# A fused attention and MLP kernel: the opening's three stages written as one list of steps, with some loads on another queue

## The chip, the cores and the metric

The kernel runs on one core of one Trainium2 chip. The metric is the device time of one execution in microseconds. Each time here is that of a whole run, or comes from the trace of one profiled execution, whose times count from the span's start.

## The reference

For 8 batches, 12 heads, 448 tokens and head size 64, cosine attention is followed by a two-layer MLP over the 3584 x 768 result:

```python
q_n = q / (np.linalg.norm(q, axis=-1, keepdims=True) + 1e-06)
k_n = k / (np.linalg.norm(k, axis=-1, keepdims=True) + 1e-06)
attn = softmax(np.matmul(q_n, k_n.transpose(0, 1, 3, 2)) / tau)
x = np.matmul(attn, v)        # heads side by side: 3584 x 768
h = x @ w_in                  # 768 x 2048
g = 0.5 * h * (1.0 + erf(h * inv_sqrt2))
return g @ w_out              # 2048 x 768
```

Inputs and output are float32; the matmuls take bf16 operands.

## The kernel before

**Work and tiles.** Four heads of a batch make a group: 3 groups a batch, 24 in all. Group 0 is split in two, so there are 25 *units*: units 0 and 1 are the halves of group 0, unit u is group u - 1 from there. A group's tokens lie as 7 chunks of 64 tokens, its heads as two pairs.

For each unit, q and k are loaded (`load_qk`, L126), squared (`square`, L151), summed over the head size on VectorE (`reduce`, L162), turned into inverse norms by a logarithm, an exponential and a reciprocal (`logs` L172, `roots` L177, `inverses` L182), multiplied by them on GpSimd into a bf16 tile (`scale`, L196), and turned round (`transposes`, L210): for the first five units on TensorE, with a copy from PSUM by VectorE (`copies`, L223), for all others by a DMA transpose on SyncE's queue. Q and K name the halves. A unit's scale can't start before its norms are there; `groups` (L117) says which units' norms are worked out together: units 5 and 6 (groups 4 and 5) share one logarithm and root.

Then come scores (`scores`, L232) into a pair of PSUM banks, exponentials on ScalarE (`exps`, L246; a visit is scores and exponential of one chunk for both head pairs, `visit`, L654), column sums by a matmul with ones (`sums`, L298), the matmul with v (`values`, L324), and the normalising into x (`turned` L341, `inverted` L346, `spread` L362, `normalise` L367).

A batch's x, 768 x 448, goes through the first layer as 16 tiles of 6 matmuls each (`w_in`, L467; tiles "hp", contraction steps kd 0 to 5, two for each group), then GELU on ScalarE into g. The second layer (`second_pieces`, L397) is a list of pieces of one matmul each (384 columns; 16 to a tile), which is used as filling between the score visits of the next batch; VectorE copies the finished tile and SyncE stores it.

**Order.** `manual_schedule` (L69) takes the program's order as each engine's order, so each engine and each queue works strictly down its own list, and waits for data and buffers only. A DMA is issued by the engine whose queue it is on: SP loads q and k and stores the output; GpSimd's queue loads v, w_in and w_out, converting to bf16 (`load_v` L141, `load_wi` L436, `load_wo` L445). `upto(f, n)` (L454) calls f for all units below n that it has not yet been called for.

The first batch has an order written out by hand, `attention_first` (L472). The first layer of each batch is `first(b)` (L863), which also holds next units' preparation; the attention of batches 1 and up is `attention(b, fill)` (L702), with a branch of its own for batch 1 (L740) and for batch 2 (L770). The counts in `parts` say how many second-layer pieces stand between visits. ScalarE needs other tables for GELU than for exponentials, so a table load stands at each change (`preload_act_table_set`).

**PSUM.** Eight banks: two single ones by turns (`mm_tile`, L102, shared by transposes, projections, pieces and fillers), two pairs for scores, and two for sums and values of the first batch, which become a third pair behind it (L961 to 963). A tile in a bank that is still being read makes TensorE wait. `qkp` has 4 buffers, so group 4's load takes group 0's.

**Fillers.** `spin(n)` (L460) is n matmuls on blank data. Before the first transposes there are 20 of them (L952) and 2 more (L495); seven others stand among the transposes, scores and the start of the first layer.

**The opening's loads.** All loads of groups 0 to 3 are issued on SP at the start, but for one on ScalarE's queue. `late` (L954) is a small copy on GpSimd that waits for group 0's last load, and so holds back GpSimd's queue. Groups 4 and 5 are loaded by SP at L507 and L535. In `attention_first` one first-layer tile, hp 4, gets its first two matmuls early (L632).

Of the kernel before, what the change touches and what calls it, by code (L numbers as in the profile page):

```python
# [16 lines left out]
def kernel(  # L17
# [17 lines left out]
    nc = tc.nc  # L35
# [90 lines left out]
    def load_qk(g):  # L126
# [137 lines left out]

    def gathered(g, p):
# [58 lines left out]
    def values(g, chunks=range(C), p=None):  # L324
        for c in chunks:
            if c == 0 and g < NQ:
# [70 lines left out]
    def second_pieces(sb, t, ni):  # L397
        state = {}

        def mm(kf):  # L400
# [8 lines left out]
            if kf == KF - 1:  # L409
                nc.vector.tensor_copy(ot[:, ni * NH:(ni + 1) * NH], ps[:, :NH])  # L410
# [7 lines left out]
        return [lambda kf=kf: mm(kf) for kf in range(KF)]  # L418
# [46 lines left out]
    early = {}  # L465

# [5 lines left out]
    def attention_first():  # L472
        x_t[0] = xp.tile([128, KD, S], BF16, tag="x", name="x0")
        DV, AC, GP = nc.vector, nc.scalar, nc.gpsimd
        Q, K = 0, 1
        square(0, ((AC, Q),))
        square(0, ((AC, K),))
        reduce(0, Q)
        reduce(0, K)
        square(1, ((AC, Q),))  # L480
        upto(load_v, 1)
        logs(0)
        reduce(1, Q)
        roots(0)
        upto(load_wi, 1)
        square(1, ((AC, K),))
        inverses(0)
        square(2, ((AC, Q),))
        reduce(1, K)
        scale(0, ((GP, 1),))  # L490
        logs(1)
        reduce(2, Q)
        roots(1)
        scale(0, ((GP, 0),))
        spin(2)  # L495
        transposes(0, 1)
        square(2, ((AC, K),))
        inverses(1)
        spin(1)
        transposes(0, 0)  # L500
        square(3, ((AC, Q),))
        copies(0, 1)
        scale(1, ((GP, 0),))
        copies(0, 0)
        square(3, ((AC, K),))
        scale(1, ((GP, 1),))
        upto(load_qk, 5)  # L507
        spin(1)
        transposes(1, 0)
        reduce(2, K)  # L510
        scores(0, ((0, 0), (0, 1)))
        upto(load_v, 2)
        transposes(1, 1)
        copies(1, 0)
        logs(2)
        scores(0, ((0, 2), (0, 3)))
        roots(2)
        upto(load_wi, 2)
        exps(0, ((0, 0), (0, 1)))
        inverses(2)  # L520
        copies(1, 1)
        exps(0, ((0, 2), (0, 3)))
        spin(2)
        scores(0, ((0, 4), (0, 5)))
        scale(2, ((GP, 0),))
        reduce(3, Q)
        exps(0, ((0, 4), (0, 5)))
        spin(1)
# [482 lines left out]
```

## Time and profile before

| what | us |
|---|---|
| median of 3 runs | 400.88 |
| the runs | 400.53, 400.88, 407.3 |
| span of the profiled execution | 398.6 |
| the median above that span | 2.28 |
| TensorE busy | 392.0 |
| ScalarE busy | 267.8 |
| VectorE busy | 264.0 |
| GpSimd busy | 250.6 |

No separate time is recorded for the profiled execution beside its span, so the 2.28 us stand for what lies around the span.

TensorE's matmuls overlap, so a busy TensorE is not always at its best; the pitch from one matmul to the next says more. In the chain that ended last each line gives the start, the length and the work. In the timeline each line gives the start, the length, the engine (PE matmul, PEld weight load, DVE VectorE, ACT ScalarE, POOL GpSimd, SPq the DMA issues of SyncE), the source line, the operation with its tiles and count, and in brackets the idle time ahead of it with what ended it. A row of DMA issues gives the size and the time from issue to landing.

### The profile page before, as it was taken

Reading aid. Unit: us, or ns where it says so; the run is one execution under the profiler, and the core shown is the slowest. Engines: PE = TensorE matmul, PEld = TensorE weight load, DVE = VectorE, ACT = ScalarE, POOL = GpSimd, SP = SyncE. Lnnn points to the kernel's source line nnn. Section 1 sums busy time; section 2 is a strip of 40 time slices with the busy share of each in tenths; the row PEclk is TensorE's granted clock in tenths of the full one; section 3 lists DMA queues with packets and bytes.
Section 4 is the critical chain, followed back from the end, with each engine's and each line's share of the span. In section 5 each row is a group of like instructions: output and inputs, shape, how many; then the busy total and the mean of one; then the engine's idle time right before and its main releaser. Section 6 shows DMA issues by size and latency. Waiting matters only on the chain.

```text
span 398.6 us, 8027 instructions
## 1 busy us (share of the span) xinstructions
PE 392.0 (98%) x3245; PEld 207.8 (52%) x3245; DVE 264.0 (66%) x530; ACT 267.8 (67%) x399; POOL 250.6 (63%) x162
## 2 busy tenths in 40 slices
PE   7999999999999999999999999999999999999996
PEld 3444555555545555555555555555555555555564
DVE  5787214955487999589963999769973797461021
ACT  6995787557988877888665977889656756504300
POOL 5898814269699694959587394969768391920000
PEclk9999999999999999999999999999999999999999
DMA  8999999747296890678145591566024720130033
GB/s 290 261 258 217 205 233 308 154 106 226 50 254 234 158 230 2 178 150 207 70 105 138 126 240 38 162 113 147 2 27 101 148 46 2 41 77 3 1 80 80
DMA packets 66485, 54.52 MB, mean 137 GB/s; under 512 B 38672, under 2 KB 62352, under 8 KB 66448
## 3 DMA queue, kind: packets, MB, share of 16 engines
q1 hardware_dynamic: 54464, 41.79, 39.0%
q0 software_dynamic: 11600, 11.80, 18.8%
q8 instruction: 25, 0.41, 0.4%
q10 hardware_dynamic: 384, 0.43, 0.3%
q14 instruction: 12, 0.10, 0.1%
HBM read 45.61 MB, written 11.01 MB: 142 GB/s over the span
## 4 chain that ended last, share of the span: by engine, by line
PE 95%; issue 1%; DVE 1%; POOL 1%; ACT 0%; POOLq 0%
PE hp L469 37%; PE op L406 36%; PE st L242 9%; PE o L320 4%; PE o L335 4%; PE op L425 1%; PE sm L305 1%; PE sh L667 1%; PE tp L221 1%; PE sm L314 1%; PE spin L463 0%; POOL wi L441 0%; DVE nq L168 0%; POOL qkb L204 0%; POOL v L145 0%
## 5 line engine op out<-in xcount | busy, mean ns | idle before, releaser
L252 ACT ACTIVATE pt<-st 128x896 bf16<-128x896 f32 x155 | 132.5, 916 | 29.0 <-PE st L242 28.4
L406 PE MATMUL op<-wo,g 128*128 128x384 bf16 x864 | 148.1, 326 | 0.0
L469 PE MATMUL hp<-x,wi 128*128 128x448 bf16 x768 | 147.0, 353 | 0.1
L204 POOL TENSOR_TENSOR qkb<-qk,rn 128x896 bf16<-128x896 f32 (+1 forms) x50 | 80.2, 1628 | 66.3 <-DVE rn L188 64.9
L406 PEld LDWEIGHTS <-g 128*128 128x128 bf16 x864 | 81.4, 98 | 62.6 <-issue 11.2
L469 PEld LDWEIGHTS <-wi 128*128 128x128 bf16 x768 | 74.4, 98 | 71.1 <-issue 2.8
L263 POOL TENSOR_TENSOR acc<-acc,pt 128x896 f32<-128x896 f32 x55 | 103.8, 1887 | 4.3
L929 ACT ACTIVATE g<-hp 128x448 bf16<-128x448 f32 x128 | 63.6, 552 | 63.6 <-PE hp L469 63.5
L410 DVE COPY ot<-op 128x384 f32<-128x384 f32 x54 | 29.9, 555 | 83.1 <-PE op L406 80.8
L168 DVE TENSOR_REDUCE nq<-sq 128x14 f32<-128x896 f32 (+1 forms) x50 | 50.6, 1038 | 10.2 <-POOL sq L160 6.7
L242 PE MATMUL st<-qkT 64*64 64x448 bf16 x620 | 46.0, 356 | 0.2 <-ACT pt L252 0.2
L160 POOL TENSOR_TENSOR sq<-qk 128x896 f32<-128x896 f32 x18 | 29.9, 1683 | 16.3 <-DMA qk<-in_q_dram 10.9
L369 DVE TENSOR_TENSOR x<-o,rs 128x448 bf16<-128x448 f32 x48 | 28.0, 609 | 9.9 <-PE sh L667 6.4
L270 DVE TENSOR_TENSOR acc<-acc,pt 128x896 f32<-128x896 f32 x30 | 33.0, 1099 | 1.0
L158 ACT ACTIVATE sq<-qk 128x896 f32<-128x896 f32 (+1 forms) x32 | 27.8, 902 | 2.2 <-DMA qk<-in_q_dram 1.8
L364 DVE STREAM_TRANSPOSE rs<-rc 128x448 f32<-128x448 f32 x48 | 28.7, 626 | 0.6
L242 PEld LDWEIGHTS <-qkT 64*64 64x64 bf16 x620 | 17.9, 105 | 20.5 <-issue 12.7
L263 POOL TENSOR_TENSOR acc<-pt 128x896 f32<-128x896 bf16 x11 | 20.7, 1879 | 8.9 <-DVE x L369 8.9
L320 PE MATMUL o<-pt,v 64*64 64x448 bf16 x364 | 24.2, 351 | 0.0
L673 ACT ACTIVATE pt<-sh 128x448 bf16<-128x448 f32 x26 | 14.1, 544 | 9.2 <-PE sh L667 8.5
L276 DVE STREAM_TRANSPOSE ta<-acc 128x448 f32<-128x448 f32 x32 | 18.5, 617 | 0.2
L335 PE MATMUL o<-pt,v 64*64 64x448 bf16 x308 | 17.5, 351 | 0.5 <-DVE x L369 0.5
(54 smaller groups left out, 212.4 us busy)
## 6 DMA issues: line engine op xcount, KB each, us to landing
qk<-in_q_dram SPq DMA_DIRECT2D x23, 448.0 KB, 4.6
qk<-in_k_dram SPq DMA_DIRECT2D x23, 448.0 KB, 5.4
out_dram<-ot SPq DMA_DIRECT2D x48, 192.0 KB, 3.2
v<-in_v_dram POOLq DMA_DIRECT2D x7, 672.0 KB, 7.7
wo<-in_moe_w_out_dram POOLq DMA_DIRECT2D x4, 768.0 KB, 11.6
wi<-in_moe_w_in_dram POOLq DMA_DIRECT2D x4, 512.0 KB, 14.4
out_dram<-ot SPq DMA_DIRECT2D x12, 96.0 KB, 2.1
wi<-in_moe_w_in_dram POOLq DMA_DIRECT2D x4, 256.0 KB, 14.6
```

The lines of the kernel that those rows point to most:

```text
L160: eng.tensor_tensor(sq, t, t, ALU.mult)
L168: nc.vector.tensor_reduce(nq_t[n][:, j, i], sq_t[g, i][:, s0:s1], mybir.AxisListType.X, ALU.add)
L204: eng.tensor_tensor(qkb[:, i, :, s0:s1].rearrange("p c s d -> p s c d"), t[:, i, s0:s1], rn[:, i].to_broadcast([128, s1 - s0, C, D]), ALU. ...
L242: nc.tensor.matmul(st[cols, n, :S], lhsT=qkT[rows, 1, c, cols], rhs=qkT[rows, 0, :, cols], start=True, stop=True, tile_position=(64 * s, 6 ...
L252: nc.scalar.activation(pt, st[:, :, :S], AF.Exp, scale=inv_tau)
L263: nc.gpsimd.tensor_tensor(acc_t[g], all_t[g][:, 0] if c == 1 else acc_t[g], all_t[g][:, c], ALU.add)
L270: nc.vector.tensor_tensor(acc_t[g], acc_t[g], all_t[g][:, c], ALU.add)
L320: nc.tensor.matmul(bank_t[g, h][64 * s:64 * (s + 1), :S], lhsT=v_t[g][rows, s, c, :], rhs=pt_t[g, s, c][rows], start=(c == 0), stop=(c == ...
L335: nc.tensor.matmul(bank_t[g, h][cols, :S], lhsT=v_t[g][rows, s, c, :], rhs=pt_t[g, s, c][rows], start=(c == 0), stop=(c == C - 1), tile_po ...
L406: nc.tensor.matmul(ps[:, :NH], lhsT=g_t[sb][:, kf, t * 128:(t + 1) * 128], rhs=wo[:, kf, ni * NH:(ni + 1) * NH], start=(kf == 0), stop=(kf ...
L469: nc.tensor.matmul(t, lhsT=wi[:, kd, m * 128:(m + 1) * 128], rhs=x_t[b][:, kd, :], start=(kd == 0), stop=(kd == KD - 1))
L929: nc.scalar.activation(g_t[sb][:, m, hf * S:(hf + 1) * S], hps.pop(m), AF.Gelu)
```

## The change

`attention_first`, the branches of `attention` for batches 1 and 2, and what `first` did for batches 0 and 1, are replaced by one function `opening()` of 594 steps, which calls the same helpers one at a time. The work is the same; what differs is the order in which each engine meets it. `first` and `attention` serve the later batches as before.

What moves, so far as the prediction speaks of it: 28 fillers (29 before), all ahead of the first transposes. The q half of unit 1 is squared on GpSimd instead of ScalarE. v is loaded behind the first part of w_in; w_in's parts come in the order 0, 2, 1, 3. `late_copy` stands behind the squares of unit 4. Groups 5 and 4 are loaded through ScalarE's queue, behind the batch's last exponential. Unit 5 (group 4) is squared on ScalarE, ahead of the first GELU, unit 6 on GpSimd. w_out's four loads are spread out. First-layer tiles 1, 0 and 2 get their banks ahead of the last sums of group 2, tile 0 in the bank that held a value tile; tile 1 also gets two matmuls there. In batch 0's first layer the GELUs come in another order than the tiles. Later, group 6's load, its square and unit 6's scale follow each other as shown.

```diff
-    def load_qk(g):
+    def load_qk(g, queue=None):
...
-                eng = nc.scalar if g == 0 and s0 == 0 and i == 1 else nc.sync
+                eng = queue or (nc.scalar if g == 0 and s0 == 0 and i == 1 else nc.sync)
...
+    def opening():
+        load_qk(0)
+        x_t[0] = xp.tile([128, KD, S], BF16, tag="x", name="x0")
+        square(1, ((GP, Q),))
+        spin(2)
+        spin(20)
+        spin(2)
+        table(EXP_SET)
+        square(0, ((AC, Q),))
+        reduce(0, Q)
+        square(0, ((AC, K),))
+        reduce(0, K)
+        square(1, ((AC, K),))
+        logs(0)
+        roots(0)
+        spin(1)
+        spin(1)
+        spin(1)
+        spin(1)
+        reduce(1, Q)
+        load_wi(0)
...
+        inverses(1)
+        scale(0, ((GP, 0),))
+        transposes(0, 0)
+        copies(0, 0)
+        load_qk(2)
+        scale(0, ((GP, 1),))
...
+        transposes(0, 1)
+        copies(0, 1)
...
+        reduce(2, K)
+        logs(2)
+        roots(2)
+        copies(1, 1)
+        load_v(0)
+        exps(0, ((0, 0), (0, 1)))
+        load_v(1)
...
+        values(1, (6,))
+        scores(2, ((0, 4), (1, 4)))
...
+        mm(0, 1, 0, 2)
...
+        logs(4)
+        roots(4)
+        exps(2, ((0, 6), (1, 6)))
...
+        values(2, (6,))
+        inverted(1)
+        load_qk(5, AC)
+        spread(1, 0)
+        banks(0, 3, 0)
+        table(GELU_SET)
+        load_qk(4, AC)
...
+        sums(2, (5,))
+        sums(2, (6,))
+        mm(0, 0, 0, 2)
...
+        square(5, ((AC, Q),))
+        square(6, ((GP, Q),))
...
+        gelu(0, 1)
+        gelu(0, 2)
+        mm(0, 5, 2, 4)
+        load_wo(1)
+        mm(0, 5, 4, 6)
+        square(5, ((AC, K),))
...
+        mm(0, 9, 2, 4)
+        transposes(4, 0)
...
+        gelu(0, 6)
...
+        table(EXP_SET)
+        logs(5)
+        roots(5)
...
+        table(GELU_SET)
...
+        inverses(5)
+        scale(5, ((GP, K),))
...
+        table(EXP_SET)
+        visit(0)
+        visit(1)
+        scale(5, ((GP, Q),))
+        visit(2)
+        run(1)
+        load_wo(2)
...
+        transposes(5)
...
+        load_qk(6)
...
+        square(7, ((AC, Q),))
...
+        load_wo(3)
+        visit(1)
+        square(7, ((GP, K),))
+        run(17)
+        scale(6, ((GP, Q),))
...
+        scale(6, ((GP, K),))
...
+        transposes(6)
+        run(3)
+        visit(1)
```

In this list `mm(b, m, k0, k1)` are the matmuls of tile m with contraction steps k0 to k1, `bank` and `banks` give tiles their PSUM banks, `run(n)` takes n second-layer pieces, `table` loads a ScalarE table, and `normalise`, `reduce` and the rest are the helpers named above.

More of the change, by code (lines that the diff above doesn't have):

```diff
@@ new lines, in attention @@
+        upto(scale, u + 5)
+        upto(transposes, u + 5)
+        upto(load_qk, g0 + 9)
+        mixed(g0, 0, (1,), (2, 1))
+        squared(u + 6, 0)
+        folded(g0 + 2, range(3))
+        run()
+        for h in range(2):
+            spread(g0 + 1, h)
+        if b + 1 < B:
+            visit(2, 0, 1)
+        else:
+            visit(2, 0)
+            weighted(g0 + 1, 1)
+            visit(2)
+        folded(g0 + 2, range(3, 6))
+        run()
+        for i in range(2):
+            reduced(u + 5, i)
@@ L884, in first @@
             bank(m)
[L885 to L898 removed]
+            mm(m, range(KD - 2))
+        if b + 1 < B:
             for n in range(3, 5):
```

939 lines of the change are left out of this document (577 added, 362 removed).

## The prediction

> **What bounds the kernel now.** I read the totals first, then the chain that ended last in order of time, then the opening instruction by instruction, then the DMA rows. The totals:
> ```profile
> span 398.6 us, 8027 instructions
> PE 392.0 (98%) x3245; PEld 207.8 (52%) x3245; DVE 264.0 (66%) x530; ACT 267.8 (67%) x399; POOL 250.6 (63%) x162
> ```
> TensorE is busy 98% of the span. Busy does not say useful, so the chain comes next, from 30 to 52 us:
> ```profile
> 30.55 0.54 PE hp L469 x2
> 31.09 0.88 PE sm L305 x8
> 31.96 0.69 PE o L335 x12
> 32.65 8.81 PE hp L469 x46
> 41.46 0.78 PE tp L221 x14
> 42.24 9.08 PE hp L469 x48
> 51.33 0.68 PE st L242 x9
> ```
> From 32.6 us the chain stays on PE, without a hole, at 0.19 us a projection matmul (9.08 / 48), to the last output piece. So behind 32.6 us a new order can win next to nothing; it can only win ahead of it, or open a hole. The opening:
> ```profile
> 5.26 0.15 PEld L463 LDWEIGHTS <-ident 128*128 128x128 bf16 x1 [0.22 <-issue]
> 5.64 1.82 PEld L463 LDWEIGHTS <-ident 128*128 128x128 bf16 x10 [0.22 <-issue]
> 8.65 0.58 PE L221 MATMUL tp<-ident,qkb 128*64 128x128 bf16 x7 [0.35 <-POOL qkb L204]
> 10.71 1.07 DVE L168 TENSOR_REDUCE nq<-sq 128x14 f32<-128x896 f32 x1
> 11.81 0.32 ACT L175 ACTIVATE lq<-nq,tiny 128x28 f32<-128x28 f32 x1 [0.32 <-DVE nq L168]
> 12.29 4.13 ACT L252 ACTIVATE pt<-st 128x896 bf16<-128x896 f32 x5
> 29.49 1.73 ACT L252 ACTIVATE pt<-st 128x896 bf16<-128x896 f32 x2 [0.55 <-PE st L242]
> 31.70 1.28 ACT L867 ACT_TABLE_LOAD   x1
> ```
> ACT sets the pace: 21 exponentials of 0.86 us from 12.29 to 31.22, with holes of 0.16 and 0.55 only. The filler matmuls start at 1.95 and come 0.37 us apart to 5.64, then 0.19. Last the DMA: its share in two-us stretches is 0.92 to 1.33 from 2 to 66 us, so landings depend on company. The same load, issued at 50 us in company and at 87 us almost alone (KB, us to landing):
> ```profile
> qk<-in_q_dram SPq DMA_DIRECT2D x1, 448.0 KB, 8.8
> qk<-in_k_dram SPq DMA_DIRECT2D x1, 448.0 KB, 10.1
> ```
> ```profile
> qk<-in_q_dram SPq DMA_DIRECT2D x1, 448.0 KB, 3.8
> qk<-in_k_dram SPq DMA_DIRECT2D x1, 448.0 KB, 4.4
> ```
>
> **The change, part by part.** Counts of matmuls, exponentials and bytes stay as they were (28 fillers for 29), so each term is a time at which something starts.
>
> (1) *Fillers ahead of the first transposes.* Before, 22 stood there, the last weight load at 7.77. Now all 28 do: 7.77 + 6 x 0.187 = 8.9, transposes at 9.1. Bounds: 7.95, when GpSimd's first scaled tile is ready (square 4.7 to 5.65, DMA issue 1.2, scale 0.95, each behind the other), if the fast pitch starts sooner; and 10.1, if each of the five added step borders costs the 0.2 seen ahead of 7.77. I take 9.1, the pitch that most rows have. Behind it on DVE: two copies at 0.62 after 0.62, then the reduction of 1.08: 9.1 + 1.86 + 1.08 = 12.04 where the trace has 11.78. Exponentials start at 12.55, **+0.26** (from -0.4 to +1.3).
>
> (2) *ACT's row.* To the last exponential's end it gains the holes (0.71) if nothing new waits. The logarithm and root of unit 4 (0.55) now come ahead of it. Scores of group 2, chunk 4, stand behind four value chunks on PE, about 0.25 of new wait. Last exponential: 31.22 + 0.26 - 0.71 + 0.55 + 0.25 = 31.57.
>
> (3) *PE behind it.* Before, projections ran on at 32.58, 1.36 later. Now only one value chunk and two sums are behind it (0.31 + 0.50): 32.38, **-0.20**. Of the three tiles begun early only one gets its two matmuls ahead of the last exponential, as one did before; the others get places, no time.
>
> (4) *Loads of groups 4 and 5 from ACT, behind the last exponential* (before from SP at 11 and 16). Two issues (0.9), the table (1.28), the third issue, 3.8 to land as at 87 us: 31.57 + 0.9 + 1.28 + 3.8 = 37.6. Behind it wait ACT's square and then every GELU. Row: square 0.95, GELUs 1 and 2 to 39.65, square to 40.6, GELUs 4, 3, 5, 0, 7 at 0.55 to 43.3. PE: 38 matmuls from 32.38 to 39.65, tile 7 finds its bank free; 6 more, transposes, 8 more to 42.85; the second transposes need tile 7's bank, wait 0.45; 18 more, then tile 12 needs tile 8's, whose GELU stands behind two table loads, waits 0.35. Projections end at 52.15 (before 51.25), **+0.90** with (3). Two us earlier landing would leave +0, 2 us later +2.5.
> The other moved loads cost nothing while these covers hold. v now stands behind wi's first part on GpSimd's queue, issued at 10.9 and 11.8: at the 354 GB/s mean of 2 to 12 us and 204 for a converting load alone it lands by 18 and 21, needed at 20 and 24. The rest of wi has 1.84 MB less ahead of it and is in by 32 (before: issued at 22.2, 14.8 to land, 37), needed from 32.8. wo's first half goes out behind GpSimd's squares of group 5 (its load lands at 35.8, square to 37.5) at 38 and 42; behind each other on the queue they land by 51, needed at 52.8. Each of these, 2 us late, would be 1 us or less of PE wait.
>
> (5) *Group 5's tile.* Roots of groups 4 and 5 at 45.7 (before 42.0), inverses 0.77, two scales to 49.85, transposes on SP. SP is in order: group 6's load follows them. GpSimd is in order too: wo's two late issues, group 6's square (1.68), and only then the two scales (3.35) and group 5's DMA transpose (3.5). SP's transpose takes 1.5 alone and 3.58 in company; at 2.5 the load is out from 52.4, its second half at 52.9. That lands 4.4 to 10.1 later. wo is in flight then, as in the row at 50, but not a second transpose: half-way, 7.2, so 60.1. Then 60.1 + 5.05 + 3.5 = 68.65. PE needs it at its 15th score visit: 52.15 + 14 visits, 65 pieces and a sum, 14.5 us = 66.65. PE waits **+2.0** (0 to 5.5). ACT's square of group 6 then ends about when its place comes, no cost.
>
> (6) *Seams.* Behind that PE's row has three more changes between small and full tiles, at 0.12 (12 score matmuls 0.69 where three visits of 0.187 are 0.56): **+0.4** (-0.5 to +1). GpSimd's squares of groups 12 and 13 hide beside PE; if not, a late transpose is next.
>
> Sum: 0.9 + 2.0 + 0.4 = 3.3 on the profiled span of 398.6, 401.9. The median of the runs is 400.88, 2.28 above that span; I carry this over: **404.2**.
>
> [...]
>
> **The rivals.**
> A. *Everything lands as if alone.* Then group 6 lands at 52.9 + 4.4, the transposes by 66, and term (5) is 0: 398.6 + 1.3 + 2.28 = 402.2 (400.5 to 402.5). For it: the weights are in by 32. Against: wo is issued into the same 10 us.
> B. *Faster.* The fast pitch comes early and the fillers end under the POOL path: exponentials at 11.9, the last at 30.9, projections at 31.7 (-0.9), and the two loads land before ACT's square costs a wait, so nothing is given back: 400.0 (399.0 to 400.5). For it: ACT's holes are really gone. Against: six fillers more; ACT's loads cannot leave before its last exponential.
> C. *Half pitch again.* With transposes and short scores alone on PE from 9 to 16 us, its matmuls take 0.37 for a stretch. One as long as the first (1.95 to 5.64) loses half of it, 1.8 on top of the forecast: 406.0 (404 to 408.5). For it: seven fillers stood there. Against: from 9.1 on my row leaves no hole over 1 us.
> D. *Slower by more than 2%.* The DMA transposes meet wo's second half: at 51.5 us one took 8.1 on SP and 12.3 to land. If group 4's issue takes 3.58 and group 6's load 10.1, and group 5's transpose 12.3, it lands at 49.9 + 3.6 + 0.5 + 10.1 + 5.05 + 12.3 = 81.4, 14.8 late: 417 (410 to 418). It decides from a landing at 75 on. For it: these very rows. Against: wo, 0.77 MB apiece, was issued twice by 51.7 and moves at 204 GB/s, so it is through by 61.
>
> **How the numbers follow.** Forecast (term 5 in some measure, 402.5 to 407) 0.43; A 0.23; B 0.20; C 0.07; D 0.07. What leaves out B's lower half and D is 399.8 to 408.5, about 0.15 outside. The forecast's own range is 402.5 to 407. Two per cent is 8.0 us, about what a measurement of this kernel tells from no change: faster would need 392.9, which not even the opening's whole hole count allows (0.01); slower needs 408.9, D and an end of C (0.08); the rest, 0.91, is within.
>
> **What would show it.** Right: first transposes at 9.0 to 9.2 with no POOL wait ahead; first exponential 12.4 to 12.8, last ends at 31.3 to 31.9; ACT idle for about 3 us on the q load of group 4, behind the table; PE waits on banks of tiles 7 and 8; at the 15th visit PE's weight load waits on a DMA transpose for 1 to 3 us; from there the old distance stays to the end. Wrong: transposes before 8.65 (1), a GELU before 38 (4), no PE wait between 53 and 70 (5), filler-free matmuls at 0.37 us (C). A wait behind 75 us that I have not named would break the sum too, as ACT's and GpSimd's rows there are new and I have bounded them by their totals only.

## The result, and the profile after

| | before | after |
|---|---|---|
| median, 6 runs each (us) | 400.98 | 417.56 |
| lowest to highest (us) | 400.53 to 407.3 | 411.74 to 423.78 |
| mean granted clock of TensorE, profiled run | 1.00 | 0.975 |
| span of the profiled run (us) | 398.6 | 422.0 |

The changed kernel is slower: ratio of the times 1.0336, 95% interval 1.0281 to 1.0391. The ratio leaves out runs more than 1.5% above the fastest of the same kernel (three of the changed kernel's six, one of the six of before), while the medians hold all runs. The profile of the changed kernel is that of the slowest of its six runs, so a size read from it is above the median's. In its six runs the time goes with the granted clock: 411.74 us at 0.992, 415.53 at 0.988, 423.78 at 0.975.

The totals of the changed kernel (busy time, share of the span, instructions):

```profile
span 422.0 us, 8023 instructions
PE 399.0 (95%) x3244; PEld 209.7 (50%) x3244; DVE 264.3 (63%) x530; ACT 270.4 (64%) x402; POOL 244.7 (58%) x159
```

TensorE is busy 399.0 us where it was busy 392.0 with one matmul more. So 7.0 us of the 23.4 are longer busy time, matmuls that ran slower, and 16.4 are idle time. ScalarE's table loads, one of 1.28 us at each change between exponentials and GELU, are good milestones (start, us):

| | before | after | difference |
|---|---|---|---|
| GELU table, behind the first batch's exponentials | 31.7 | 41.4 | 9.7 |
| exponential table, ahead of batch 1's visits | 51.9 | 62.2 | 10.3 |
| exponential table, ahead of batch 2's visits | 98.0 | 118.8 | 20.8 |
| GELU table, first layer of batch 2 | 134.5 | 155.5 | 21.0 |
| end | 398.6 | 422.0 | 23.4 |

Nearly all of the loss thus sits in two places: before 41 us, and in batch 1 (62 to 119 us). A small rest of 2.4 us comes behind 155 us.

**The first place.** TensorE's instructions in the opening of the changed kernel (start, length, engine, line, operation; in brackets the idle time and what ended it):

```profile
1.95 8.24 PE L468 MATMUL spin<-g,ident 128*128 128x448 bf16 x28 [1.95 <-DVE root L92]
10.25 0.94 PE L221 MATMUL tp<-ident,qkb 128*64 128x128 bf16 x14
20.69 1.76 PE L242 MATMUL st<-qkT 64*64 64x448 bf16 x8 [6.18 <-ACT pt L252]
```

The fillers end at 10.2, so the first transposes start at 10.25 (before 8.65). Then TensorE stands for 6.18 us. ScalarE says why:

```profile
12.80 0.95 ACT L158 ACTIVATE sq<-qk 128x896 f32<-128x896 f32 x1 [1.51 <-DMA qk<-in_q_dram]
18.42 0.95 ACT L158 ACTIVATE sq<-qk 128x896 f32<-128x896 f32 x1 [4.67 <-DMA qk<-in_k_dram]
19.74 1.71 ACT L252 ACTIVATE pt<-st 128x896 bf16<-128x896 f32 x2
```

The same square in the kernel before, ahead of its first exponential at 12.29:

```profile
10.54 0.95 ACT L158 ACTIVATE sq<-qk 128x896 f32<-128x896 f32 x1 [0.31 <-DMA qk<-in_k_dram]
```

ScalarE's list is in order. The square of group 2's k stands ahead of the first exponential, and its load landed 14.7 us after its issue (6.8 in the profile of before). The first exponential starts at 19.74, 7.45 later than before, though its scores had long been there. In the windows of two us (busy time and count of PE, PEld, DVE, ACT, POOL, then granted clock, DMA share, GB/s):

```profile
14.00:16.00 2.00, 0.52 (x9) 0.46 (x8) 0.13 (x1) 0.00 (x0) 0.88 (x2) 0.86 1.09 247
16.00:18.00 2.00, 0.00 (x0) 0.00 (x0) 0.00 (x0) 0.00 (x0) 0.00 (x0) 0.50 1.06 233
20.00:22.00 2.00, 1.31 (x8) 0.48 (x7) 1.83 (x4) 1.76 (x3) 1.40 (x1) 0.50 0.41 70
26.00:28.00 2.00, 2.00 (x14) 0.56 (x11) 0.62 (x1) 0.92 (x1) 1.99 (x4) 0.50 0.01 1
28.00:30.00 2.00, 2.00 (x20) 0.81 (x19) 0.39 (x1) 0.99 (x2) 2.00 (x3) 0.72 1.10 200
72.00:74.00 2.00, 1.34 (x9) 0.70 (x10) 0.31 (x1) 0.91 (x1) 0.00 (x0) 0.87 1.17 270
74.00:76.00 2.00, 2.00 (x13) 0.76 (x15) 0.25 (x1) 0.96 (x2) 0.00 (x0) 0.50 1.17 283
76.00:78.00 2.00, 2.00 (x20) 0.82 (x13) 0.00 (x0) 1.86 (x3) 0.57 (x1) 0.78 1.10 192
```

From 15.4 to 29.1 us (0.86 and 0.72 are windows that are partly at half) the clock is at half, so PE is "busy" 2.00 of 2.00 in the window from 26 us with only 14 matmuls: seven transposes take 0.93 us at 25.40 and 0.56 at 29.81, at full clock. Busy does not say useful. The profile of before has a clock of 1.00 in all these windows, as here:

```profile
16.00:18.00 2.00, 2.00 (x25) 1.01 (x23) 1.56 (x4) 1.97 (x5) 0.88 (x2) 1.00 1.10 248
```

**The second place.** TensorE's two long waits in batch 1:

```profile
72.66 0.38 PE L242 MATMUL st<-qkT 64*64 64x448 bf16 x4 [4.31 <-DMA qkT<-qkb]
85.89 0.38 PE L242 MATMUL st<-qkT 64*64 64x448 bf16 x4 [2.94 <-DMA qkT<-qkb]
```

They are the scores of group 4 (8th visit) and of group 5 (15th). The DMA issues from 59 to 64 us, with KB and us to landing:

```profile
wo<-in_moe_w_out_dram POOLq DMA_DIRECT2D x2, 768.0 KB, 18.1
qk<-in_q_dram SPq DMA_DIRECT2D x1, 448.0 KB, 13.1
qk<-in_k_dram SPq DMA_DIRECT2D x1, 448.0 KB, 14.9
qkT<-qkb SPq DMA_TRANSPOSE x1, 13.3
```

w_out's second half, group 4's transpose and group 6's load go out within three us and all land 13 to 18 us later. Group 4's transpose is late by itself. Group 5's is late because GpSimd's square ahead of its scales waits for group 6's k:

```profile
59.21 1.81 POOL L453 DMA_DIRECT2D wo<-in_moe_w_out_dram  x2
77.42 1.68 POOL L160 TENSOR_TENSOR sq<-qk 128x896 f32<-128x896 f32 x1 [16.41 <-DMA qk<-in_k_dram]
79.07 3.33 POOL L204 TENSOR_TENSOR qkb<-qk,rn 128x896 bf16<-128x896 f32 x2
```

The windows from 72 us shown above have the price of such a wait: it is followed by some us at half clock. Waits of 4.31 and 2.94 and two stretches of half clock worth 1.7 each make 10.7, where the milestones say 10.5.

### The profile page after: what moved, and what is told of

Read it like the earlier page. It is cut to its first block, busy times and chain, and to the rows that moved or that the text cites. A ratio compares the mean times of both kernels' runs of the same rounds, so it can differ in the third digit from the quotient of the medians.

```text
span 422.0 us, 8023 instructions
## 1 busy us (share of the span) xinstructions
PE 399.0 (95%) x3244; PEld 209.7 (50%) x3244; DVE 264.3 (63%) x530; ACT 270.4 (64%) x402; POOL 244.7 (58%) x159
## 4 chain that ended last, share of the span: by engine, by line
PE 61%; POOL 9%; DVE 4%; DMA 4%; issue 2%; ACT 1%; SPq 0%; POOLq 0%; DVEq 0%
PE hp L472 25%; PE op L411 24%; POOL acc L263 5%; PE st L242 4%; PE o L325 3%; POOL qkb L204 3%; PE o L340 2%; DMA qkT<-qkb 2%; DMA qk<-in_k_dram 1%; PE op L430 1%; POOL sq L160 1%; DVE ta L281 1%; PE sh L518 1%; DMA qk<-in_q_dram 1%; DVE sa L283 1%
## 5 line engine op out<-in xcount | busy, mean ns | idle before, releaser
L411 PE MATMUL op<-wo,g 128*128 128x384 bf16 x864 | 150.1, 328 | 0.0
L242 PE MATMUL st<-qkT 64*64 64x448 bf16 x620 | 49.8, 374 | 14.5 <-DMA qkT<-qkb 7.5
L158 ACT ACTIVATE sq<-qk 128x896 f32<-128x896 f32 (+1 forms) x35 | 31.3, 918 | 16.7 <-DMA qk<-in_q_dram 11.8
L160 POOL TENSOR_TENSOR sq<-qk 128x896 f32<-128x896 f32 (+1 forms) x15 | 24.3, 1630 | 26.8 <-DMA qk<-in_k_dram 18.3
L325 PE MATMUL o<-pt,v 64*64 64x448 bf16 x364 | 24.2, 351 | 0.0
L524 ACT ACTIVATE pt<-sh 128x448 bf16<-128x448 f32 x26 | 14.1, 543 | 10.1 <-PE sh L518 9.4
```

The costliest lines, as they stand in the source:

```text
L158: eng.activation(sq, t, AF.Square)
L242: nc.tensor.matmul(st[cols, n, :S], lhsT=qkT[rows, 1, c, cols], rhs=qkT[rows, 0, :, cols], start=True, stop=True, tile_position=(64 * s, 6 ...
L325: nc.tensor.matmul(bank_t[g, h][64 * s:64 * (s + 1), :S], lhsT=v_t[g][rows, s, c, :], rhs=pt_t[g, s, c][rows], start=(c == 0), stop=(c == ...
L411: nc.tensor.matmul(ps[:, :NH], lhsT=g_t[sb][:, kf, t * 128:(t + 1) * 128], rhs=wo[:, kf, ni * NH:(ni + 1) * NH], start=(kf == 0), stop=(kf ...
```

## The experiments

My first theory was that w_in's first part, now ahead of v on GpSimd's queue, holds back the k load of group 2, and that all else follows from the late opening. Its rival was that the second place has a cause of its own. Times are medians, ratios are against the kernel before on the same chip.

**v ahead of w_in again, and w_in moved far back.**

```diff
 (first run)                      (second run)
+        load_v(0)                -        load_wi(0)
         load_wi(0)                ...
 ...                                       load_v(1)
-        load_v(0)                +        load_wi(0)
```

> The changed kernel with v's small first load put ahead of w_in's first load on GpSimd's queue; nothing else differs. Theory A (w_in's long rows, first on that queue from 5.8 us, take the DMA engines from the loads of groups 1 and 2, and ScalarE stands behind the last of them): the k load of group 2 lands at 11 to 14 us instead of 18.4, the first exponential starts at 13 to 15.5 instead of 19.7, and the time falls by 4 to 9 us, to 404 to 411. Rival 1 (all of GpSimd's traffic slows them alike, what counts is that it starts 0.6 us earlier than before): the landing stays at 17 to 19 and the time at 412 to 418. Rival 2 (the loss sits in the late DMA transposes behind 60 us): the first exponential may move, the time falls by under 2 us.

> The changed kernel with w_in's first load moved behind v's two loads, about 6 us later on GpSimd's queue. Theory A: nothing competes with the loads of groups 0 to 2, the k load of group 2 lands at 10 to 11 us, the first exponential starts at 12.5 to 13 (28 fillers end at 10.2 here), and the time falls by 8 to 12 us, to 402 to 408; w_in's first part still lands before its use near 30. Rival 2 (late transposes set the loss): the time falls by under 2 us. Rival 3 (the DMA time put off now comes back later): the first exponential is early, but the first projections wait for w_in, and half of the gain is lost.

Measured: 416.69 us (1.0405, 1.0388 to 1.0422) and 417.07 (1.0409, 1.0392 to 1.0427). In both profiles k of group 2 lands in time (8.8 and 6.9 us after its issue), the 6 us hole is gone and the first exponential starts at 13.84 and 14.14. The time doesn't fall, and waits of 1.93 and 3.74 (2.38 and 3.64) us for the two DMA transposes are there. So the second place doesn't need the late opening: that part of my theory fell.

**The same exchange in the kernel before.**

```diff
-        upto(load_v, 1)
+        upto(load_wi, 1)
         ...
-        upto(load_wi, 1)
+        upto(load_v, 1)
```

> The kernel before with only v's first load and w_in's first load exchanged on GpSimd's queue. Theory A: the k load of group 2 lands at 15 to 18 us instead of 10.4, the first exponential starts 4 to 8 us later than 12.3, and the time rises by 4 to 10 us, to 405 to 411. Rival 1 (what counts is the start of the queue's traffic, not what is first): the landing stays below 12 and the time within 1 us of 401.

Measured: 401.54 us (1.0036, 0.9999 to 1.0072). The order of w_in and v by itself adds 0.7 us at the median, with an interval from 0 to 2.9. In the one profile k came after 9.4 us and the clock was at half from 16 to 26, and four of the ten runs have a clock of 0.990 or less (403.9 to 410.0 us), where one of the thirteen of the kernel before beside them has; the other six took some 401 us at full clock. In later runs with the changed kernel's queue order the same load took 6.7, 7.9, 7.9, 12.4, 12.7 and 15.0 us. So the order alone doesn't say where the load lands. Whether it makes a late landing more likely is taken up below, under what stays open.

**Thirty fillers into the hole.**

```diff
         transposes(1, 0)
+        spin(30)
         exps(0, ((0, 4), (0, 5)))
```

> The changed kernel with 30 more filler matmuls on TensorE behind the transposes of unit 1, where it stood idle from 14.5 to 20.7 us. The late load stays. If the half pitch from 21 to 29 us comes from that idle time, the pitch stays full there and the batch's projections start 1.5 to 3.5 us earlier than 42.2: 409 to 416 at the median, and the runs scatter less than from 411.7 to 423.8. If the half pitch costs nothing since ScalarE sets the pace there, the time stays where it was, within 1 us.

Measured: 421.34 us (1.0512, 1.0479 to 1.0545). Inconclusive on the hole: in the profile the load came after 7.9 us, there was no hole to fill, and the fillers held up TensorE. The clock stayed at 1.00 through the opening.

**Group 5's scales ahead of the waiting square.** In GpSimd's list, and so the DMA transpose behind them on SP.

```diff
+        scale(6, ((GP, Q),))
+        scale(6, ((GP, K),))
         square(7, ((GP, K),))
 ...
-        scale(6, ((GP, Q),))
 ...
-        scale(6, ((GP, K),))
```

> The changed kernel with GpSimd's two scales of unit 6 ahead of its square of unit 7, so that they no longer wait for group 6's load. Theory B (the prediction's term 5: TensorE waits 3 to 5 us at the 15th visit since group 5's transpose stands behind that load on GpSimd, and then runs 3 us of work at half pitch): the transpose is issued at 53 to 57 us instead of 71 to 82, the wait at the 15th visit goes, and the time falls by 5 to 8 us below the changed kernel's 412 to 418. Rival (the two transposes and w_out's second half in one stretch only slow each other): the transpose lands 10 to 13 us after its issue but still in time, the wait at the 8th visit grows by 1 to 3 us, and half of the gain is lost.

Measured: 414.72 us (1.031, 1.0245 to 1.0375). TensorE's waits of this run in batch 1:

```profile
64.16 0.38 PE L242 MATMUL st<-qkT 64*64 64x448 bf16 x4 [2.28 <-DMA qkT<-qkb]
74.23 3.04 PE L411 MATMUL op<-wo,g 128*128 128x384 bf16 x9 [2.47 <-DMA wo<-in_moe_w_out_dram]
```

Group 5's transpose is in time now. In its place the second-layer pieces wait for w_out itself. A wait was moved.

**w_out's second half right behind its first; or behind both pairs of scales.**

```diff
 (first run)                      (second run)
         load_wo(0)                        scale(5, ((GP, Q),))
+        load_wo(2)                 ...
+        load_wo(3)                +        scale(6, ((GP, Q),))
                                   +        scale(6, ((GP, K),))
                                   +        load_wo(2)
                                   +        load_wo(3)
                                            square(7, ((GP, K),))
```

> The changed kernel with w_out's second half issued right behind its first half, some 8 us earlier, so it is mostly through when group 4's transpose and group 6's load start. If company with w_out is what makes those two late (10 to 13 us to land instead of 3.5 and 4.4): they land 2 to 4 us sooner, the waits at the 8th and 15th visits shrink together by 3 to 6 us, time 407 to 413. If only the order on GpSimd counts: within 2 us of the changed kernel.

> The changed kernel with unit 6's scales right behind unit 5's, and w_out's second half behind them. Theory B with company: group 4's transpose and group 6's load go out alone at about 50 to 52 us and land after 3.5 to 6; group 5's transpose lands by 62; both waits go, and with them the half pitch: 9 to 12 us below the changed kernel, 402 to 406. What is then left over the kernel before is the late start of the exponentials and about 2 us behind 150 us. If w_out then comes late for its pieces near 66 us: a new wait of 1 to 3 us there.

Measured: 417.16 (1.0377, 1.0305 to 1.0449) and 414.63 (1.029, 1.0209 to 1.0371). In the first, TensorE waits 3.95 us for group 4's transpose, and for nothing else over 1 us in batch 1. In the second both transposes are in time and w_out is 3.06 late. In the second the loads of group 6 are issued ahead of w_out, and land so:

```profile
qk<-in_q_dram SPq DMA_DIRECT2D x1, 448.0 KB, 3.9
qk<-in_k_dram SPq DMA_DIRECT2D x1, 448.0 KB, 5.0
```

The same loads took 13.1 and 14.9 beside w_out's second half. Three orders, and in each TensorE waits for one or another of these transfers. So the new question was why those transfers are there so late at all.

**The fillers back among the transposes and scores.** The changed kernel with 20 and 2 ahead of the first transposes, and the other six one or two at a time at five later places, much as before.

```diff
-        spin(2)
         spin(20)
-        spin(2)
 ...
-        spin(1)      (four times)
 ...
+        spin(2)
         transposes(0, 0)
 ...
+        spin(1)      (at five further places 1, 1, 2, 1, 1)
```

> The changed kernel with its 28 fillers where the kernel before had them: 20 and 2 ahead of the first transposes, six among the transposes and first scores. Term 1 of the prediction: the first transposes start at 8.2 to 8.7 instead of 10.25, and the first exponential 0.5 to 1.8 us sooner where the load of group 2 is not late. Rival C (half pitch without the fillers between): the pitch stays full from 14 to 24 us. Both together 1 to 4 us below the changed kernel; if the loads set the start, under 1 us.

Measured: 411.49 us (1.024, 1.0172 to 1.0309), 6 less than the changed kernel, and more than the 1 to 4 expected. First exponential at 11.84, last one's end 30.92, projections from 31.78: with its fillers where they were, the new order's opening is 0.3 to 0.8 us better in this profile than in that of before, and its clock is 1.00 up to 68 us. The waits in batch 1 stay:

```profile
58.37 0.38 PE L242 MATMUL st<-qkT 64*64 64x448 bf16 x4 [0.88 <-DMA qkT<-qkb]
65.97 1.89 PE L411 MATMUL op<-wo,g 128*128 128x384 bf16 x9 [0.26 <-DMA wo<-in_moe_w_out_dram]
71.60 0.59 PE L242 MATMUL st<-qkT 64*64 64x448 bf16 x4 [3.73 <-DMA qkT<-qkb]
```

**Four runs to part the two places.** In the kernel before, GpSimd issues w_out's halves at 30.0 and 40.2 us, the first ahead of group 3's scales, the second ahead of those of groups 4 and 5. In the changed kernel with its fillers back they go out at 36 to 40 and 48.3 us, with the same row of the first layer. From here on the theory was that this delay is the second place's cause (theory W). Rival letters hold for the run that they stand in.

```diff
 the kernel before, w_out late             the kernel before, fillers ahead
-        upto(load_wo, 2)                   scale(0, ((GP, 0),))
 ...                                       -        spin(2)
-            upto(load_wo, 4)              +        spin(9)
+            upto(load_wo, 2)               ...
 ...                                       -        spin(1)  (and 1, 2, 1, 1, 1)
                 upto(transposes, u + 2)
                 if b == 0:
+                    upto(load_wo, 4)
```

> The kernel before, with w_out's four loads as late as the change has them: the first two behind group 6's squares' place in the first layer (about 40 us), the other two behind the scales of groups 4 and 5 (about 50 us). Nothing else is touched. Theory W (what the change loses behind 60 us comes from w_out being issued 8 to 9 us later against the row of the first layer, so that its second half lies on the DMA transposes and on group 6's loads): PE waits of 2 to 5 us for w_out or for a DMA transpose appear between 55 and 75 us, where the kernel before has none, with some us at half clock behind them, so 404 to 409 us. Rival S (the change's order of steps on GpSimd is the cause, scales behind a square that waits, and w_out's place is only company): no wait over 1 us, 401 to 402 us. The opening must be unchanged: first exponential at 12.3, first-layer row at 32.6.

Measured: 409.41 us (1.0178, 1.0095 to 1.0261); three of the four runs took 407.9 to 409.6, the fourth 417.5. The opening has its old order, though in this profile the first exponential starts at 13.68 (+1.4). Then one wait, and the clock behind it:

```profile
69.66 2.72 PE L406 MATMUL op<-wo,g 128*128 128x384 bf16 x8 [4.32 <-DMA wo<-in_moe_w_out_dram]
```

```profile
66.00:68.00 2.00, 0.00 (x0) 0.00 (x0) 0.00 (x0) 0.00 (x0) 0.75 (x1) 1.00 1.23 187
68.00:70.00 2.00, 0.34 (x2) 0.17 (x2) 0.00 (x0) 0.00 (x0) 0.00 (x0) 0.60 1.24 193
70.00:72.00 2.00, 2.00 (x8) 0.81 (x6) 0.00 (x0) 0.00 (x0) 0.00 (x0) 0.50 1.25 181
72.00:74.00 2.00, 2.00 (x22) 0.59 (x24) 0.56 (x1) 1.05 (x2) 0.00 (x0) 0.50 1.16 141
74.00:76.00 2.00, 2.00 (x36) 0.88 (x32) 0.84 (x2) 1.48 (x2) 0.31 (x1) 0.69 1.05 360
```

The milestone ahead of batch 1's visits is 1.4 us later than in before, the one ahead of batch 2's 8.8, and from there to the end 8.8 stays. So moving w_out alone makes a second place in the kernel before, of 7.4 us. Here the wait is for w_out itself, and in the changed kernel for the transposes beside it. In the other direction:

> The changed kernel with the fillers back in their old places (as in the run that gave 411.5 us) and with w_out's first half ahead of group 3's scales on GpSimd's queue (about 30 us) and its second half behind the v load of batch 1 (about 40 us), as the kernel before has them. Theory W: the waits of 0.88, 0.26 and 3.73 us for DMA transposes and w_out between 58 and 72 us are gone, and with them about 2.5 us of half clock: 7.4 us less than that run's 411.5, so 404 (402.5 to 406). Rival S: group 5's transpose still stands behind the square that waits for group 6's loads, so a wait of 2 us or more stays at the 15th visit: 407 to 411. Rival A (loads of groups 4 and 5 through ScalarE's queue now meet w_out and land 3 us later): a PE wait of 2 to 4 us between 40 and 50 us, in which ScalarE waits for its square, 406 to 408.

Edit: `load_wo(0)` and `load_wo(1)` ahead of `scale(4, ...)`, `load_wo(2)` and `load_wo(3)` behind `load_v(2)`, on top of the fillers back. Measured: 412.2 us (1.0251, 1.0164 to 1.0338). Not one wait for w_out or a transpose is left between 50 and 80 us, as theory W has it. But the time is no better, as the run's rival A has it: the q and k loads of groups 4 and 5, issued by ScalarE at 41 us in this profile, now run beside w_out and land after 8.7 and 10.5 us in the median (4.9 and 5.6 in the changed kernel), and the GELUs behind their square are late:

```profile
53.80 2.40 PE L472 MATMUL hp<-x,wi 128*128 128x448 bf16 x6 [3.98 <-ACT g L501]
```

This profile is that of the longest of the four runs (421.13 us), in which k of group 2 landed after 15.0 us. That the same wait stands in the other three, 410.98 to 413.42 us, is not shown.

> The run before this one, with the q and k loads of groups 3, 4 and 5 on SyncE's queue in the kernel before's places (about 3, 11 and 16 us) in place of ScalarE's queue at 31 to 35 us. Theory W alone: as that run, within 0.7 us, since the waits for those loads on ScalarE cost the first layer 0.1 to 0.6 us. Rival A: 2 us or more faster than that run, and ScalarE's square of group 4 starts without a wait. Against a gain: SyncE's early loads meet w_in and v in the first 25 us, and a v or w_in that lands late would show as a PE wait before 35 us.

```diff
         load_qk(2)
+        load_qk(3)
 ...
         scale(1, ((GP, 0),))
+        load_qk(4)
 ...
         scale(2, ((GP, 0),))
+        load_qk(5)
 ...
-        load_qk(3)
 ...
-        load_qk(5, AC)
 ...
-        load_qk(4, AC)
```

Measured: 407.0 us (1.0124, 1.0017 to 1.023), some 5 less than the run before it, as rival A has it. Group 3's load goes out on SyncE's queue at 4.4 us in the changed kernel too, so what moves is the loads of groups 4 and 5 (to 16 and 21.5 us in this profile). So w_out's place gains only together with theirs: loads that go out of ScalarE's queue some 20 us later leave no room for w_out in time. The loads of groups 4 and 5 back alone, with w_out late, were not tried. Left are 1.75 us of wait for w_in at 34.38 and 1.64 for group 5's transpose at 69.44.

> The kernel before with its nine small fillers moved ahead of the first transposes; nothing else is touched. Theory F (the fillers between transposes and scores hold the clock, and ahead of the transposes they cost their own time): first transposes at 10 to 10.7 in place of 8.65, first exponential near 13.8 in place of 12.29, then some us at half clock between 13 and 25, row of the first layer at 34 to 36 in place of 32.6: 402.5 to 404.5 us. Rival (the fillers ahead of the transposes are hidden under GpSimd's path and those between do nothing): 400.4 to 401.4, full clock throughout.

Measured: 403.72 us (1.0089, 1.0044 to 1.0133). First transposes at 9.86 for 8.65, first exponential 13.10 for 12.29, first-layer row at 34.34 for 32.59, clock 0.56 and 0.58 in the windows from 16 to 20, of which the first is

```profile
16.00:18.00 2.00, 2.00 (x19) 1.06 (x17) 1.53 (x3) 1.67 (x4) 1.33 (x1) 0.56 1.10 248
```

All ten runs have a clock of 0.991 to 0.995. Two of the nine fillers of the expectation stood ahead of the first transposes already, so the edit moves seven: their place is worth 2.9 us in a kernel where nothing else is touched. This profile also has a wait of 3.71 us for a DMA transpose, and is 4 us over the median; the run's own median is the better number.

**Three more, on how the two add up and on the rest.**

> The changed kernel, its fillers where the change has them, with w_out and the q and k loads of groups 3 to 5 in the kernel before's places. If fillers and loads cost independently: 417.6 less the 4.5 us between the runs with 411.5 and 407.0, so 413 (411.5 to 414.5), with an opening late by 1.5 to 8 us, half clock in it, and no wait over 2 us between 55 and 85 us. Rival (the late opening moves the score visits away from the loads, so that putting the loads back gains nothing): 416 to 418. Rival (the earlier q and k loads take the opening's own loads further back): over 419.

Edit: the two edits on w_out and on the q and k loads, with the fillers where the change has them. Measured: 412.01 us (1.0243, 1.0163 to 1.0323); 413 was expected. Two waits for transposes, 1.10 and 2.32 us, stay in batch 1, where none over 2 was expected. Fillers and loads add up within 1.1 us, which is less than the runs of one cell lie apart:

| median, us | loads as changed | loads as before |
|---|---|---|
| fillers as changed | 417.56 | 412.01 |
| fillers as before | 411.49 | 407.0 |

The fillers' place is worth 5.0 to 6.1 us by this table, the loads' place 4.5 to 5.6.

> The run with fillers, w_out and the q and k loads of groups 3 to 5 in the kernel before's places (407.0 us), and two steps more: the scales of group 5 ahead of group 6's K square on GpSimd, and the last part of w_in ahead of group 3's squares on GpSimd's queue. Theory W: the waits of 1.64 us (transpose of group 5) and 1.75 us (w_in) go, nothing new comes: 403.3 to 404. Rival S' (each load moved earlier makes another one late, since the queue is full from 2 to 60 us): the same sum of waits under other names, 406 to 408.

Edit: on top of fillers and loads as before, `scale(6, ...)` ahead of `square(7, ...)`, and `load_wi(3)` right behind `load_wi(1)`. Measured: 406.98 us (1.0113, 0.9998 to 1.0229), runs at a clock of 0.999 or more 404.45 and 405.96. The 1.64 is gone and the 1.75 is 0.96, but this profile's opening ends 1.9 us later than that run's (33.60 for 31.70). The median lies in the rival's range, the two runs at full clock between it and the expectation; the step is too small for these runs.

> The run before this one, with the two squares of group 12 on ScalarE, as in the kernel before, in place of GpSimd. Theory G (GpSimd's running sums of group 8 end 24 us later because these squares stand between them, so that the inverse norms and PE's waits of 0.84 and 0.41 us in the third batch come from it): those waits go, 1.3 us less than the run before this one, 402 to 402.7. Rival: those waits belong to VectorE's own longer list; no difference within 0.4 us, or 1 us slower if ScalarE's exponentials wait behind the squares.

```diff
-        square(13, ((GP, K),))
+        square(13, ((AC, K),))
 ...
-        square(13, ((GP, Q),))
+        square(13, ((AC, Q),))
```

Measured: 407.68 us (1.0097, 1.0042 to 1.0152), but the ten runs lie in two clusters: 402.53, 402.77, 402.98 and 404.6 at clock 1.00, and six from 407.5 up at 0.992 or less. The median isn't lower than that of the run before, so the expectation holds for the runs at full clock only: they are about 2 us below the two of the run before. The trace agrees with the theory: the waits of 0.58 and 0.40 us behind 160 us, which the run before it has,

```profile
164.21 0.57 PE L242 MATMUL st<-qkT 64*64 64x448 bf16 x8 [0.58 <-DVE x L374]
181.95 3.38 PE L472 MATMUL hp<-x,wi 128*128 128x448 bf16 x17 [0.40 <-DVE ot L415]
```

are not in it, and the distance to before grows by 0.2 us from the first layer of batch 2 to the end (11.8 to 12.0) where it grows by 1.9 in the run before (3.5 to 5.4) and by 2.4 in the changed kernel. That is the small rest. No version of these beats the kernel before; most of its runs at full clock (400.3 to 401.1) are 2 us under the best of them. The new opening with all else as before was not tried; by the one profile it could gain 0.3 to 0.8 us, and two profiles with the old order differ by 1.4 in their first exponential (12.29 and 13.68).

## Why the prediction was wrong

I forecast 404.2 us, with a range from 399.8 to 408.5; it is 417.56. The parts of the change that I named are the ones that cost. Two steps failed. Term (1) priced the fillers' new place at +0.26 us, and the runs put it at 5.0 to 6.1 (2.9 in the kernel before), since the clock falls besides. Terms (4) and (5) priced the moved loads at nothing "while these covers hold" and at +2.0, and the runs put them at 4.5 to 5.6.

The mechanisms of rivals C and D, 7 in 100 each, both came true. That D's number was 417 is luck: D has 14.8 us at the 15th visit, where the profile has a wait of 2.94, one of 4.31 at the 8th, and 9.7 us in the opening, which D doesn't have.

- **(1) Fillers ahead of the transposes.** Forecast 9.1, bounds 7.95 to 10.1; measured 10.25 (9.86 in the kernel before with only this edit). I took the pitch of most rows, 0.187, for the added ones. The weight loads show that those that stand as steps of their own come some 0.4 apart:

```profile
8.03 0.28 PEld L468 LDWEIGHTS <-ident 128*128 128x128 bf16 x2 [0.31 <-issue]
8.63 0.10 PEld L468 LDWEIGHTS <-ident 128*128 128x128 bf16 x1 [0.31 <-issue]
9.03 0.10 PEld L468 LDWEIGHTS <-ident 128*128 128x128 bf16 x1 [0.31 <-issue]
9.44 0.10 PEld L468 LDWEIGHTS <-ident 128*128 128x128 bf16 x1 [0.31 <-issue]
10.12 0.91 PEld L221 LDWEIGHTS <-qkb 128*64 128x64 bf16 x14 [0.58 <-issue]
```

 The 0.31 ahead of each is what stands ahead of 7.77 in the kernel before, too. I had taken it as 0.2, and for the upper bound only, so that even the bound of 10.1 is passed. The rest of the step is not in this sum at all: it is rival C's clock. With the loads as before, the profile with the fillers ahead is 2.3 us behind the one with the fillers between at the first exponential (14.09 for 11.76) and 4.9 at the GELU table (35.70 for 30.85), with a stretch of half clock between.

- **(2) and (3) ScalarE's row and TensorE behind it.** Forecast: last exponential 31.57, projections 32.38. With the fillers back they are 30.92 and 31.78: right in size and even low on the gain. In the changed kernel's profile they are 41.33 and 42.19, 10 us late. Of these, 7.45 stand at the first exponential already, behind the k load; the rest comes with the half clock, as ScalarE then waits for scores (0.24 to 0.93 us at a time). In the five runs with the fillers ahead, k in time and nothing added between, the first exponential is at 13.10 to 14.14. What failed is the sentence "if nothing new waits". ScalarE's squares of group 2 stand ahead of the first exponential, in both kernels, and I didn't name the load that they wait for.

- **(4) Loads through ScalarE.** Forecast 1.1, from -0.20 to +0.90; measured 0.6 between the two milestones (9.7 to 10.3). The landing of 3.8 that I took was 4.9 and 5.6 in the median. Right as far as TensorE's own waits go, and the covers of v and w_in held: no wait for them stands in this profile (the mean of 2 to 12 us that I used is 344 GB/s and not 354, which moves nothing here). What I called covered, w_out behind GpSimd's squares that wait for these very loads, was the step that broke: I had w_out's first half at 38 and 42 and its second half behind it, and asked only whether TensorE would need them in time.

- **(5) Group 5's tile.** The chain was right, link for link: GpSimd's square waits for group 6's k, then come the scales, then the transpose. The size failed, and so did the link ahead of it. I took 7.2 us to land for group 6's load; 13.1 and 14.9 were measured, though the same load in company had stood at 8.8 and 10.1. And I gave group 4's own transpose no term; it landed after 13.3 us and cost 4.31. The ground on which I set D aside was that w_out "moves at 204 GB/s, so it is through by 61". That is the failing step: I let w_out have the DMA engines alone, while in the same sum group 4's transpose and group 6's load went out beside it. It took 18.1 us to land, to 78; with the 10 us by which this profile is late, that is 68 against my 61.

- **(6) Seams.** Forecast 0.4. The 2.4 us behind 155 us are of another kind: GpSimd's squares of group 12, which I said "hide beside PE; if not, a late transpose is next". What was next, by the trace with these squares on ScalarE, was a running sum and the normalising behind it.

- **Rival C.** I priced one stretch of half clock at 1.8 us and doubted that there would be a hole. The price was right: with the fillers ahead in the kernel before the opening loses one such stretch, 1.7 us. The number of stretches was not. A long wait in batch 1 brought one or two (3.4 us behind the one wait of 4.32 in the kernel before with w_out late), and in the opening the clock fell without a hole as well (no wait over 0.95 us with group 5's scales ahead of the square).

**What stays open.** Why k of group 2 lands after 6.7 us in one run and after 14.7 in another of the same queue order. I dropped the order of v and w_in as a cause too soon. In the five profiles with v ahead of w_in the load took 6.8 to 8.8 us; of the twelve with w_in ahead, six have 6.6 to 8.3 and six 9.4 to 15.0. That is a hint and not shown: fillers and loads as before with v ahead of w_in in the new order was not run.

The clock of each run says more than one profile does. In the kernel before, 38 of 45 runs whose clock was noted beside the experiments are at 0.999 or more (leaving out one of 812.48 us), and the other seven, 405.3 to 407.4 us, at 0.982 to 0.996. In the changed kernel none of six is at 0.999, and in the three kernels with fillers and loads both put back 8 of 18 are. So what is left of the change still makes a fall of the clock more frequent; which step does it is open.

## What to carry over

A filler's place counts: in the kernel before, with seven short matmuls between real work, the clock reads 1.00; with the same seven in a row ahead of it the first transposes are 1.2 us later, the clock reads 0.56 and 0.58 from 16 to 20 us, and the run takes 2.9 us more. Here w_out's second half, moved behind the first layer, went out within three us of a transpose and of group 6's load, and all of them landed after 13 to 18 us; so ask of each moved transfer who shares the DMA engines with it when it now runs, and price all of them at the landing times of the busiest rows. In batch 1 of these profiles each wait of 2.9 us or more on TensorE cost more than its length: add the half-clock stretch that followed, 1.7 or 3.4 us.

## What the runs showed of the hardware

**The clock lost comes in multiples of one amount in these profiles.** The time that the clock took away, two us times (1 - clock) summed over the windows of a stretch, is 3.42 in the kernel before with w_out late (0.40, 0.50, 0.50 and 0.31 of four windows), 6.84 in the opening of the changed kernel, and in the other profiles with a fall 1.7, 3.4, 5.1 or 8.5: multiples of 1.71, which is half clock for 3.42 us. No window reads less than 0.50. Where TensorE stood idle in part of such a stretch, less than this sum shows in its busy time: in the changed kernel the sums of its three stretches up to 92 us (6.84, 1.70 and 1.72) make 10.3, and its busy time is 7.0 us longer. The first microseconds are not in these windows: the fillers come 0.37 us apart to 5.64 and 0.19 from there, and the clock reads 1.00 in both.

The waits of 3.64 to 4.32 us in batch 1 each have a fall that begins within 2 us of their end. Of the waits of 2.28 to 3.06 us there, four have one (2.32, 2.47, 2.94 and 3.06) and two have not (2.28 and 2.38). So in this range the length of the wait alone doesn't decide; what does is not shown.

The opening shows a fall without such a wait. With group 5's scales ahead of the square, no wait of TensorE behind the fillers is over 0.95 us in the opening, and yet the clock is at half from 15.4 on (2 us windows as above):

```profile
12.00:14.00 2.00, 1.45 (x16) 0.87 (x16) 1.83 (x4) 1.54 (x4) 0.84 (x2) 1.00 1.06 246
14.00:16.00 2.00, 1.36 (x8) 0.37 (x7) 1.94 (x4) 1.97 (x3) 1.65 (x1) 0.84 1.07 244
16.00:18.00 2.00, 1.94 (x14) 1.19 (x15) 1.25 (x4) 1.51 (x4) 1.69 (x2) 0.50 1.09 261
```

All profiles together: with fillers between and k of group 2 landing within 8.8 us of its issue the clock stays full in the opening (before, and four other runs); with k after 9.4 us or more it falls wherever the fillers are (six runs); with the fillers ahead and k within 8.8 us it falls in four runs of six, and one of the other two is the run with thirty fillers put in. With group 5's scales ahead, TensorE was busy with transposes and short scores for 1.45 and 1.36 us of the two windows from 12 us, about 70%, and the clock fell; with v ahead of w_in again it was busy for 0.97 us in the window from 14 us, and the clock stayed full. What tells the two apart was not measured.

**One transfer's landing time went with its neighbours.** The 448 KB load took 3.9 us where w_out was held back and 13.1 beside it; a DMA transpose took 3.4 us nearly alone (at 82 us in the changed kernel) and 13.3 in company, and the load through ScalarE's queue went from 4.9 to 8.7 when w_out was put beside it. These transfers stand on three queues, w_out on GpSimd's, the transposes and group 6's load on SyncE's, groups 4 and 5 on ScalarE's: in these rows another engine's queue gave no room of its own.
